# Weights converted in 8 units, one FFN product also on GpSimd, tiles 0 to 2 visited in a snake, v halves by DMA, two blocks' y in one pair of banks, and a new order of all tasks

## The chip, the cores and the metric

One NeuronCore of one Trainium2 chip runs the whole program. The metric is the device time of one execution in microseconds (us). The kernel before took 539.49 us (median of three runs, 539.39 to 540.33).

The engines go by short names: PE is TensorE (matmul; PEld its weight loads), DVE is VectorE, ACT is ScalarE, POOL is GpSimd, SP is SyncE, which here only issues DMAs. Each engine works through its own queue in program order, and they meet at semaphores.

## What is computed

A linear attention with a decaying state, and behind it a feed-forward network (FFN) with a rational activation. The reference, cut:

```
for t in range(S):                                   # B,H,S,D = 4,8,768,48
    cur = einsum('bhd,bhe->bhde', u * kt, vt)
    y[:, :, t] = einsum('bhd,bhde->bhe', rt, state + cur)
    state = w[..., None] * state + einsum('bhd,bhe->bhde', kt, vt)
x = y as (3072 tokens, 384)
h = x @ w_in                                         # 384 x 2048
g = (a0 + a1*h + a2*h^2 + a3*h^3) / (1 + |b0|*|h| + |b1|*h^2 + 1e-6)
out = g @ w_out                                      # 2048 x 384
```

The weights `w_in` and `w_out` come as float64, 6.3 MB each.

## The kernel before, in words

**Attention.** The tokens are cut into 24 blocks of 128 (4 sequences, 6 blocks each; block n is block n // 4 of sequence n % 4). For each block k, r and v are loaded (`Lk`, `Lr`, `Lv`), k is scaled by inverse powers of the decay (`sk`), k and r are transposed on PE (`tk`, `tr`) and evicted (`tke`, `tre`). PE then makes the scores and the state update in two banks (`akv`), with matmuls on 64x64 quarters of the array. DVE masks the scores (`ae`, four per block), the state is moved on (`kvm`, `kvx`, `ca`), PE makes y (`y`) and DVE adds it to a bonus term (`ye`). The bonus term is built by `ba`, `bb`, `bs`, `bv`. `LV` makes a copy of v whose halves of 64 rows stand exchanged, either by an engine from v in SBUF or by a DMA from DRAM (line 451).

**FFN.** Two blocks are a tile of 256 tokens; there are 12. y is transposed (`x`) and split into a high and a low part (`xh`, `xl`). The hidden width of 2048 is cut into 16 pieces of 128, and a slice is four such pieces of one tile: 48 slices, the last one split (list `SL`, line 35). For a slice, `f1` makes h (36 matmuls of 256 columns, into PSUM buffer h0 or h1), ACT makes `z`, `t`, `q`, `ln`, `ex`, DVE makes `u3`, `hi`, `p`, `d`, `lo`, each one pass over 128x1024 elements, and `f2` multiplies the high and low part of g with `w_out` (two halves of 12 matmuls of 384 columns). `p` (line 683) is (q + QE) * hi, `d` uses it, and `lo` is the last that reads the slice's PSUM buffer, so the slice two further on that uses the buffer waits for `lo`. Runs of slices that follow one another in one tile (`VISIT`, line 44) collect in one PSUM bank per half; at the end of a run `os` evicts it, the first time as a copy, later by adding to the sum in SBUF (lines 735 to 745).

**Weights.** Each weight is turned from float64 into a high and a low float32r part by `cl` (load), `c0` (scale the upper word, line 378), `cu` (the lower word), `c2` (shift, line 385), `c3` (sign, line 388), `cr` (integer add, line 392), `ch` (high part, line 397) and `co` (low part, line 400). This is done in 28 pieces: 12 of `w_in` (128x512) and 16 of `w_out` (128x384). Tiles 0 to 2 are worked together on the first half of the hidden width, since the later weights are not there yet.

**The order.** A string `ORDER` (lines 49 to 162) names every task, its engine (D, A, G for POOL, P, S) and its buffer; the program issues them in this order, which is so the order of each engine's queue. `warm.n` issues n matmuls of 512 bf16 columns whose result is not used (line 782). At the end a flag (`flag`, `flagt` on PE, `flagm` on DVE, lines 354 and 355) says whether a general path must run instead; every engine loads it at line 891 and branches at line 892.

```
for task in ORDER.split():
    task, e, slot = re.fullmatch(r"(.+)([A-Z])((?:[a-z]+\d)*)", task).groups()
    name, *at_ = task.split(".")
    here[:] = re.findall(r"[a-z]+\d", slot)
    FN[name](ENG[e], *at_)
```

Of the kernel before, what the change touches and what calls it, by code (L numbers as in the profile page):

```python
# [49 lines left out]
pad.0G mskG pad.1G Lr.1A wS cl_D ctrA plGos0 pow.0D inv.2Dta0 inv.3D inv.0D warm.10P turn.0.1Ppa0 pow.1D turn.2.1P turn.3.1P  # L50
inv.1D Lk.0Slx0 Lr.0S pow.2D pow.3D tr.0Ph0 turn.1.1P tab.1A sk.0D warm.4P tk.0Ph1 tre.0D Lv.0Sldv0 LV.0.0Avx0 LV.0.1A Lv.1Sldv1
cl.3S c0.3A c2.3Dpa1 Lk.1Slx1 Lk.2Slx2 sk.1G tr.1Ppa0 tke.0A warm.1P akv.0Ph0 tre.1D c3.3D w128D ba.1Dm0 ba.0Gm1 tk.1Ph1 cl.1S
tke.1A c0.1A cu.1A Lr.2S warm.3P akv.1Ph1 pad.2G ae.0.1.0D sk.2G tk.2Ppa0 kvm.0D kvx.0D ae.0.0.0D ae.0.1.1D ae.1.0.0D ae.0.0.1D
warm.2P warm.13P y.0Ph0 ae.1.1.0D ba.2Dm2 cl.0S c0.0A tke.2A kvm.1D c2.1Dpa1 c2.0Dpa0 c3.0D c3.1D uwS bb.1G Lk.3Slx0 cl.2S cu.2A
cu.0A Lr.3S Lv.2Sldv2 c0.2A ae.1.0.1D kvx.1D bb.0G bb.2G LV.1.0Avx1 LV.1.1A cr.1Gta1 ch.1A bs.0Ddt0 bv.0G bs.1Ddt1 ae.1.1.1D
tr.2Ppa0 c2.2Dpa1 c3.2D tre.2D ye.0D sk.3G tk.3Ppa1 warm.1P akv.2Ph1 cl.8S cr.0Gta2 c0.8A LV.2.0Avx2 LV.2.1A c2.8Dpa0 ae.2.1.0D
bs.2Ddt0 c3.8D Lk.4Slx1 cl.4S cl.21S co.1G cr.2Gta3 ch.0A kvm.2A c0.4A cu.3A kvx.2D ch.2A c2.4Dpa0 ae.2.0.0D ae.2.0.1D c3.4D
# [111 lines left out]
def tile_linear_attention_rational_ffn(ctx, tc, r, k, v, w, u, w_in, w_out, a, b, out):  # L169
# [195 lines left out]
    def wo_of(j, part):  # L365
        return whole["o", j][:, part]
# [557 lines left out]
```

## Time and profile before

| | |
|---|---|
| median of three runs | 539.49 us |
| span of the profiled execution, first to last instruction (the time that the profile has of it) | 536.8 us |
| PE busy | 516.8 us (96%), 6174 matmuls |
| DVE busy | 472.0 us (88%), 654 instructions |
| ACT busy | 345.9 us (64%), 421 instructions |
| POOL busy | 149.0 us (28%), 166 instructions |
| share of the chain that ended last: PE, DVE, DMA | 79%, 9%, 3% |

A median run is 2.7 us longer than the profiled span. Busy time of an engine is the union of its instructions; the time from one matmul's start to the next one's start is shorter than the duration shown for one, since matmuls are pipelined, and DVE's instructions overlap a little too. A row of a group ends with the idle time ahead of the group and what ended it.

### The profile page before, as it was taken

What the parts mean: (1) busy time and instruction counts of PE and PEld (TensorE: products, weight loads), DVE (VectorE), ACT (ScalarE), POOL (GpSimd) and SP (SyncE); (2) the same over time, 40 slices, a digit from 0 to 9 for tenths busy, and PEclk for the clock granted to TensorE, in tenths of its full rate; (3) what the DMA queues carried; (4) which work ended last, traced back from release to release, by engine and by line L of the source; (5) the groups of instructions that cost most, each with busy time, mean ns of one, the idle gap of its engine ahead of it and who ended that gap; (6) DMA issues with size and microseconds to landing.
All of it is one profiled execution on the core that took longest, in us unless ns stands there. A gap on an engine that the chain in (4) does not pass through costs nothing.

```text
span 536.8 us, 14270 instructions
## 1 busy us (share of the span) xinstructions
PE 516.8 (96%) x6174; PEld 488.5 (91%) x6174; DVE 472.0 (88%) x654; ACT 345.9 (64%) x421; POOL 149.0 (28%) x166
## 2 busy tenths in 40 slices
PE   7689999999999999999999999999999999999996
PEld 4466799989999999999999999999999999999995
DVE  6889999999999999898899898899769898798675
ACT  3578999876765655743566565575665746656663
POOL 3788954858513030014320210005002000000000
PEclk9999999999999999999999999999999999999999
DMA  9999910600043310161212420022000010010101
GB/s 196 267 267 321 236 54 2 129 1 3 0 83 60 80 29 1 34 126 23 49 32 46 94 63 5 16 45 50 16 18 1 2 42 2 1 46 1 44 2 35
DMA packets 90358, 33.93 MB, mean 63 GB/s; under 512 B 83504, under 2 KB 86704, under 8 KB 90288
## 3 DMA queue, kind: packets, MB, share of 16 engines
q1 hardware_dynamic: 88960, 32.36, 24.6%
q8 instruction: 50, 0.82, 0.6%
q10 hardware_dynamic: 1328, 0.59, 0.4%
q14 instruction: 20, 0.16, 0.1%
HBM read 28.22 MB, written 4.72 MB: 61 GB/s over the span
## 4 chain that ended last, share of the span: by engine, by line
PE 79%; DVE 9%; DMA 3%; ACT 2%; issue 1%; SPq 0%; DVEq 0%; ACTq 0%
PE h L618 34%; PE o L622 11%; PE o L624 11%; PE o L623 11%; DMA swi<-in_moe_w_in_dram 3%; PE y L569 2%; PE akv L519 2%; PE y L567 2%; PE akv L523 1%; PE tk L497 1%; PE tr L497 1%; PE x L593 1%; DVE q L685 1%; DVE h L676 1%; DVE g L681 1%
## 5 line engine op out<-in xcount | busy, mean ns | idle before, releaser
L618 PE MATMUL h<-xthi,wi 128*128 128x256 f32 x1152 | 216.0, 282 | 1.4 <-DVE l L694 1.1
L618 PEld LDWEIGHTS h<-xthi,wi 128*128 128x128 f32 x1152 | 180.3, 188 | 3.6 <-issue 1.2
L618 PE MATMUL h<-xtlo,wi 128*128 128x256 f32 x576 | 160.7, 279 | 0.0
L622 PE MATMUL o<-wo,g 128*128 128x384 f32 x384 | 133.1, 347 | 0.0
L623 PE MATMUL o<-wo,g 128*128 128x384 f32 x384 | 129.1, 336 | 0.0
L624 PE MATMUL o<-wo,l 128*128 128x384 f32 x380 | 128.1, 337 | 0.4 <-DVE l L694 0.3
L618 PEld LDWEIGHTS h<-xtlo,wi 128*128 128x128 f32 x576 | 108.3, 188 | 0.0
L664 ACT ACTIVATE z<-h,off,root 128x1024 f32<-128x1024 f32 (+1 forms) x48 | 57.3, 1194 | 65.4 <-PE h L618 55.3
L681 DVE SCALAR_TENSOR_TENSOR g<-h,sig,z 128x1024 fp32r<-128x1024 f32 (+1 forms) x48 | 61.0, 1271 | 28.4 <-ACT z L672 27.9
L655 ACT ACTIVATE q<-h 128x1024 f32<-128x1024 f32 (+2 forms) x50 | 49.3, 989 | 53.2 <-PE h L618 42.1
L622 PEld LDWEIGHTS o<-wo,g 128*128 128x128 f32 x384 | 72.2, 188 | 1.0
L624 PEld LDWEIGHTS o<-wo,l 128*128 128x128 f32 x380 | 71.4, 188 | 1.0 <-DVE l L694 1.0
L623 PEld LDWEIGHTS o<-wo,g 128*128 128x128 f32 x384 | 72.3, 188 | 0.0
L668 ACT ACTIVATE z<-q,sig 128x1024 f32<-128x1024 f32 (+1 forms) x48 | 54.9, 1144 | 26.6 <-DVE h L676 25.6
L676 DVE SCALAR_TENSOR_TENSOR h<-z,sig,h 128x1024 f32<-128x1024 f32 (+1 forms) x48 | 61.1, 1272 | 7.1 <-ACT z L664 3.8
L685 DVE SCALAR_TENSOR_TENSOR q<-q,sig,g 128x1024 f32<-128x1024 f32 (+2 forms) x50 | 64.4, 1289 | 1.4
L689 DVE SCALAR_TENSOR_TENSOR h<-h,sig,q 128x1024 f32<-128x1024 f32 (+2 forms) x50 | 62.4, 1248 | 1.3
L659 ACT ACTIVATE q<-q,off,root 128x1024 f32<-128x1024 f32 (+2 forms) x50 | 60.4, 1207 | 0.8
L694 DVE TENSOR_TENSOR l<-h,z 128x1024 fp32r<-128x1024 f32 (+1 forms) x48 | 58.1, 1211 | 2.3 <-DVE h L689 0.5
L478 POOL TENSOR_TENSOR m<-rh,kn 128x384 f32<-128x384 f32 x20 | 23.8, 1193 | 113.7 <-DMA kn<-in_k_dram 66.2
L672 ACT ACTIVATE z<-z 128x1024 f32<-128x1024 f32 (+1 forms) x48 | 50.5, 1052 | 1.5
L530 DVE TENSOR_TENSOR sc<-akv,mask 64x256 f32<-64x256 f32 x96 | 40.4, 421 | 5.1 <-PE akv L523 3.2
(132 smaller groups left out, 672.7 us busy)
## 6 DMA issues: line engine op xcount, KB each, us to landing
swo<-in_moe_w_out_dram SPq DMA_DIRECT2D x16, 384.0 KB, 6.6
swi<-in_moe_w_in_dram SPq DMA_DIRECT2D x12, 512.0 KB, 6.6
kn<-in_k_dram SPq DMA_DIRECT2D x24, 192.0 KB, 4.1
vn<-in_v_dram SPq DMA_DIRECT2D x24, 192.0 KB, 3.8
rh<-in_r_dram SPq DMA_DIRECT2D x23, 192.0 KB, 3.6
out_dram<-os SPq DMA_DIRECT2D x22, 192.0 KB, 2.1
vx<-in_v_dram SPq DMA_DIRECT2D x26, 48.0 KB, 2.7
out_dram<-os ACTq DMA_DIRECT2D x2, 192.0 KB, 2.8
```

The lines of the kernel that those rows point to most:

```text
L618: nc.tensor.matmul(o, wi_of(j, cc, part), x_[:, cc], start=(n == 0), stop=(n == 3 * NCC - 1))
L622: nc.tensor.matmul(o, hi, wo_of(j, HI), start=first, stop=False)
L623: nc.tensor.matmul(o, hi, wo_of(j, LO), start=False, stop=False)
L624: nc.tensor.matmul(o, lo, wo_of(j, HI), start=False, stop=last)
L659: nc.scalar.activation(g["q"], g["q"], AF.Square, scale=RB, bias=KB)
L664: nc.scalar.activation(g["t"], g["h"], AF.Square, scale=RA, bias=KA)
L668: nc.scalar.activation(g["z"], g["q"], AF.Ln, bias=QE)
L676: nc.vector.scalar_tensor_tensor(g["h"], g["t"], KAP, g["h"], op0=ALU.add, op1=ALU.mult)
L681: nc.vector.scalar_tensor_tensor(g["hi"], g["h"], c0, g["z"], op0=ALU.add, op1=ALU.mult)
L685: nc.vector.scalar_tensor_tensor(g["q"], g["q"], qe, g["hi"].bitcast(F32), op0=ALU.add, op1=ALU.mult)
L689: nc.vector.scalar_tensor_tensor(g["h"], g["h"], c0, g["q"], op0=ALU.add, op1=ALU.subtract)
L694: nc.vector.tensor_mul(g["lo"], g["h"], g["z"])
```

## The change

Five things, and a new `ORDER`:

1. Weight conversion in 8 units (w_in and w_out in four groups of 512 hidden columns each; even units are w_in, odd w_out), each 1536 columns wide. A task names unit, part and number of parts: thirds of 512 or halves of 768 columns. `c0` may run on POOL, `ch` and `co` on DVE.
2. A task `qa` on ACT adds QE to q, and `p` of slices 0, 1, 15, 19 and 40 is then a plain product on POOL.
3. `SL` visits (2,0) (2,4) (1,4) (0,4) (0,8) (0,12) instead of (2,0) (0,4) (1,4) (2,4) (0,8) (0,12), a snake through tiles 0 to 2.
4. A task `Y` makes y of both blocks of a tile in one pair of banks, used for tiles 4 to 10.
5. More of the `LV` halves come by DMA.

Tasks by engine in the two orders, where they differ (counted from the strings):

```
               before             after
c0             A 28               A 9, G 8
cu             A 28               A 17
c2, c3         D 28 each          D 24 each
cr             G 28               G 16
ch             A 28               A 15, D 1
co             G 28               G 15, D 1
cl             S 28               S 20
p / qa         D 50 / -           D 45, G 5 / A 5
os             A 20, D 16         A 16, D 16
LV             A 16, D 6, S 26    A 4, D 8, S 36
kvm            A 2, D 22          A 4, D 20
xh             A 15, D 9          A 18, D 6
tke            A 20, D 4          A 19, D 5
sk             D 4, G 20          D 7, G 17
bb / bv        D 3, G 21 / D 7, G 17     D 4, G 20 / D 6, G 18
ca             D 4, G 16          D 7, G 13
y / Y          P 24 / -           P 10 / P 7
warm           81 matmuls         34 matmuls
```

The flag's tasks `flagt` and `flagm` stand ahead of slice 48 before, and at the very end after. The core of the diff:

```diff
-    (0, 0, 4), (1, 0, 4), (2, 0, 4), (0, 4, 4), (1, 4, 4), (2, 4, 4), (0, 8, 4), (0, 12, 4), (1, 8, 4),
+    (0, 0, 4), (1, 0, 4), (2, 0, 4), (2, 4, 4), (1, 4, 4), (0, 4, 4), (0, 8, 4), (0, 12, 4), (1, 8, 4),
...
+hi.1Dta5
+f2.0.1P cr.2.0.2Gta4 Lv.8Sldv2 c3.3.2.3D os.0.0Aos1 p.1G f1.2.0Ph1 cl.4.1.3S ch.2.0.2A ch.2.1.2A cu.6.1.2A Lr.6S co.2.1.2G co.2.0.2G
+c2.3.1.3Dpa1 f1.2.1P f1.2.2P f1.2.3P c2.3.0.3Dpa0 c3.3.1.3D c3.3.0.3D d.1D c0.4.0.2G t.2Ata0 z.2Ata2 lo.1Dta3 f1.3.0Ph0 Lr.7S q.2A
...
+hi.49D d.48D p.49D lo.48D d.49D f2.47.0P f2.47.1P lo.49D f2.48.1P f2.49.1P f2.48.0P f2.49.0P os.49.1Aos2 od.11.1A os.49.0Aos4 od.9.1S
+flagtPh0 od.11.0A flagmD
...
+    QW = NCC * CW
+    def cols(k, m):
+        return ts(k, QW // m)
...
+    def cv_exp(c, k, m, e):
+        top = c["top"][:, cols(k, m)].bitcast(F32)
+        if e is nc.scalar:
+            e.activation(top, top, AF.Copy, scale=2.0 ** -112)
+        else:
+            e.tensor_scalar(top, top, 2.0 ** -112, None, op0=ALU.mult)
...
+    def cv_round(c, k, m):
+        bits = ew.tile([P, QW // m], I32, tag=here[0], name=f"b{c['tag']}_{k}")
+        nc.gpsimd.tensor_tensor(bits, c["top"][:, cols(k, m)], c["low"][:, cols(k, m)], op=ALU.add)
+        c["f", k] = bits.bitcast(F32)
...
+    def yy_pe(f):
+        both = pair("y", 2 * f)
+        wide = state[2 * f].pop("yw", None)
+        for x in range(2):
+            n, o = 2 * f + x, x * NP * D
+            state[n]["y"] = tuple(bank[:, o : o + NP * D] for bank in both)
+            if wide is not None:
+                state[n]["yw"] = wide[:, :, o : o + NP * D]
+            y_pe(n)
...
-    def ew_p(s, qe=QE):
+    def ew_qa(s):
         g = gs[s]
+        nc.scalar.activation(g["q"], g["q"], AF.Identity, bias=QE)
+
+    def ew_p(s, qe=QE, e=None):
+        g = gs[s]
+        if e is nc.gpsimd:
+            e.tensor_mul(g["q"], g["q"], g["hi"].bitcast(F32))
+            return
         nc.vector.scalar_tensor_tensor(g["q"], g["q"], qe, g["hi"].bitcast(F32), op0=ALU.add, op1=ALU.mult)
```

## Rows read from the trace of the kernel before

**Rows 1.** Three stretches; columns: stretch, length, each engine's busy time, granted clock, DMA, GB/s
```profile
core 0: us, PE busy (x) PEld busy (x) DVE busy (x) ACT busy (x) POOL busy (x), PEclk, DMA share, GB/s
0.00:125.50 125.50, 111.38 (x1495) 92.58 (x1495) 115.47 (x198) 98.82 (x164) 84.97 (x100) 0.99 0.60 158
125.50:242.20 116.70, 116.70 (x1358) 114.30 (x1351) 109.15 (x152) 71.07 (x73) 29.36 (x30) 1.00 0.22 48
242.20:531.50 289.30, 288.70 (x3333) 281.67 (x3331) 246.72 (x306) 175.86 (x186) 34.64 (x38) 1.00 0.12 28
```

**Rows 2.** Instructions in order of time, DVE and PE, around the start of slice 8
```profile
124.30 1.22 DVE L694 TENSOR_TENSOR l<-h,z 128x1024 fp32r<-128x1024 f32 x1
...
125.45 0.22 PE L567 MATMUL y<-vn,sc 64*64 64x48 f32 x1
125.60 0.39 PE L618 MATMUL h<-xthi,wi 128*128 128x256 f32 x1
```

**Rows 3.** Instructions in order of time, PE, the last matmul
```profile
531.19 0.33 PE L624 MATMUL o<-wo,g 128*128 128x384 f32 x1
```

**Rows 4.** Instructions in order of time, PE, 47 to 53 us: fillers, transposes
```profile
47.22 2.32 PE L782 MATMUL idle_bank<-wones 128*128 128x512 bf16 x10
...
50.92 0.63 PE L497 MATMUL tk<-ident,kh 128*128 128x128 f32 x4
```

**Rows 5.** DVE's groups by shape, first 126 us: count, busy us, mean ns
```profile
L530 DVE TENSOR_TENSOR sc<-akv,mask 64x256 f32<-64x256 f32 x32 | 13.5, 421 | 2.5 <-PE akv L523 1.9
...
L685 DVE SCALAR_TENSOR_TENSOR q<-q,sig,g 128x1024 f32<-128x1024 f32 x7 | 9.6, 1366 | 0.1
...
L385 DVE TENSOR_SCALAR c<-swo 128x384 int32<-128x384 int32 x15 | 8.2, 554 | 0.5 <-issue 0.2 <-ACT swo L378 0.2
...
L385 DVE TENSOR_SCALAR c<-swi 128x512 int32<-128x512 int32 x12 | 8.0, 685 | 0.1
...
L745 DVE SCALAR_TENSOR_TENSOR os<-o,sig,os 128x384 f32<-128x384 f32 x4 | 2.4, 605 | 0.0
```

**Rows 6.** Instructions in order of time, DVE, two neighbours
```profile
54.01 0.69 DVE L385 TENSOR_SCALAR c<-swi 128x512 int32<-128x512 int32 x1
54.60 0.55 DVE L580 TENSOR_TENSOR m<-y,m 128x384 f32<-128x384 f32 x1
```

**Rows 7.** POOL by line: low parts (min/median/max ns), integer add (count, busy, mean ns)
```profile
L400 POOL TENSOR_TENSOR wo<-bwo,wo x16: 992/1018/2006, 40.5 to 139.3; 128x384 fp32r<-128x384 f32 x16
L400 POOL TENSOR_TENSOR wi<-bwi,wi x12: 1267/1295/2253, 24.5 to 110.7; 128x512 fp32r<-128x512 f32 x12
...
L392 POOL TENSOR_TENSOR bwi<-swi 128x512 int32<-128x512 int32 x12 | 12.5, 1040 | 5.9 <-PE o L624 3.8 <-issue 1.1 <-POOL bwo L392 0.9
```

**Rows 8.** Instructions in order of time, DVE and POOL side by side near 110 us
```profile
109.92 1.89 DVE L685 SCALAR_TENSOR_TENSOR q<-q,sig,g 128x1024 f32<-128x1024 f32 x1
110.70 2.25 POOL L400 TENSOR_TENSOR wi<-bwi,wi 128x512 fp32r<-128x512 f32 x1
```

**Rows 9.** Instructions in order of time, DVE, the end of slice 1
```profile
73.54 1.21 DVE L694 TENSOR_TENSOR l<-h,z 128x1024 fp32r<-128x1024 f32 x1
```

**Rows 10.** Three more stretches, columns as in the first group
```profile
0.00:10.00 10.00, 6.61 (x27) 3.26 (x28) 5.14 (x16) 3.30 (x7) 2.17 (x15) 1.00 0.93 177
20.00:30.00 10.00, 6.34 (x127) 4.38 (x126) 7.71 (x16) 6.44 (x15) 7.53 (x8) 0.83 0.94 236
0.00:74.75 74.75, 62.96 (x989) 46.02 (x990) 66.06 (x133) 54.44 (x105) 54.88 (x71) 0.98 0.90 241
```

**Rows 11.** DMA issues: count, KB each, median us to landing
```profile
vx<-in_v_dram SPq DMA_DIRECT2D x26, 48.0 KB, 2.7
```

**Rows 12.** The flag on DVE in order of time; line 892 on PE (ns, start us)
```profile
523.15 0.27 DVE L354 TENSOR_REDUCE oks<-flagt 1x1 f32<-1x128 f32 x1
523.45 0.14 DVE L355 CAST okf<-oks 1x1 int32<-1x1 f32 x1
...
L892 PEldq COMPARE_BRANCH  x1: 3322/3322/3322, 531.1 to 531.1; - x1
```

**Rows 13.** Instructions in order of time, PE, after the longest early wait
```profile
24.16 1.02 PE L497 MATMUL tk<-ident,kh 128*128 128x128 f32 x4 [3.65 <-DVE swi L388]
```

More of the change, by code (lines that the diff above doesn't have):

```diff
@@ L54 @@
[L54 to L57, printed above, removed]
@@ L358, in tile_linear_attention_rational_ffn @@
     HI, LO = 0, 1
-    pieces = []
+    units = []
     whole = {}
+    QW = NCC * CW
     def wi_of(j, cc, part):
-        return whole["i", j * P // CW, cc][:, part, ts(j % (CW // P), P)]
+        return whole["i", j * P // CW][:, part, ds(cc * CW + j * P % CW, P)]
     def wo_of(j, part):
-        return whole["o", j][:, part]
-    def piece(name, src, n):
-        pieces.append({"name": name, "src": src, "n": n, "tag": "w" + "_".join(map(str, name))})
-    def cv_load(c, e):
-        st = cst.tile([P, c["n"], 2], I32, tag=c["tag"], name="s" + c["tag"])
-        e.dma_start(st.rearrange("p n two -> p (n two)"), c["src"])
-        c["top"], c["low"] = st[:, :, 1], st[:, :, 0]
@@ L390, in cv_round @@
-    def cv_round(c):
-        bits = ew.tile([P, c["n"]], I32, tag=here[0], name="b" + c["tag"])
-        nc.gpsimd.tensor_tensor(bits, c["top"], c["low"], op=ALU.add)
-        c["f"] = bits.bitcast(F32)
-    def cv_hi(c):
-        c["w"] = whole[c["name"]] = cst.tile([P, 2, c["n"]], F32R, tag=c["tag"], name=c["tag"])
-        nc.scalar.copy(c["w"][:, HI], c["f"])
-    def cv_lo(c, e):
-        e.tensor_sub(c["w"][:, LO], c["f"], c["w"][:, HI].bitcast(F32))
+        return whole["o", j * P // CW][:, part, ts(j % (CW // P), DM)]
@@ new lines, in cols, with cv_load @@
+    def cols(k, m):
+        return ts(k, QW // m)
+    def cv_load(c, k, m, e):
+        if "st" not in c:
+            c["st"] = cst.tile([P, QW, 2], I32, tag=c["tag"], name="s" + c["tag"])
+            c["top"], c["low"] = c["st"][:, :, 1], c["st"][:, :, 0]
+        dst = c["st"][:, cols(k, m)].rearrange("p n two -> p (n two)")
+        kind, g = c["name"]
+        if kind == "i":
+            e.dma_start(dst, wi32[ts(k, P), ts(g, 2 * CW)])
+        else:
+            j = CW // P // m
+            rows = ds((g * m + k) * j * P, j * P)
+            e.dma_start(dst.rearrange("p (j n) -> p j n", j=j), wo32[rows, :].rearrange("(j p) n -> p j n", p=P))
@@ L408, in tile_linear_attention_rational_ffn @@
     for g in range(FF // CW):
-        for cc in range(NCC):
-            piece(("i", g, cc), wi32[ts(cc, P), ts(g, 2 * CW)], CW)
-        for j in range(g * (CW // P), (g + 1) * (CW // P)):
-            piece(("o", j), wo32[ts(j, P), :], DM)
+        for kind in "io":
+            units.append({"name": (kind, g), "tag": f"w{kind}{g}"})
     rh, kh, rt, sc, vs = ([], [], [], [], [])
@@ L464, in pair @@
         if here[0][0] == "h":
-            wide = state[n][nm + "w"] = ps_h.tile([P, GW], F32, tag=here[0], name=f"{nm}{n}")
+            wide = ps_h.tile([P, GW], F32, tag=here[0], name=f"{nm}{n}")
+            state[n][nm + "w"] = wide.rearrange("t (x c) -> t x c", x=2)
             return wide[:, 0:512], wide[:, 512:1024]
```

261 lines of the change are left out of this document (133 added, 128 removed).

## The prediction

> **What bounds the kernel now.** I read three things in order: where TensorE (PE) is full, who holds it up before that, and what it does at the end. Busy time by stretch [rows 1]: from 125.5 us on PE is busy for all of 116.7 us and for 288.7 of 289.3; only the first 125.5 us have room (111.4, and filler matmuls are in it). In that stretch VectorE (DVE) is busy 115.5 of 125.5. The seam is exact [rows 2]: DVE finishes the low half `lo` of slice 6 at 124.30 + 1.22 = 125.5, which frees the PSUM buffer h0, and PE starts slice 8 (into h0) at 125.60, right behind the last y matmul. From there to its last matmul [rows 3] PE needs 531.19 + 0.33 - 125.60 = 405.9 us with next to no waiting. So the time is: DVE's ordered work up to `lo` of slice 6 (DVE is an in-order queue), then 405.9 us of PE, then an end of 536.8 - 531.5 = 5.3 us. The sum below is made against this execution's span of 536.8; the median, 539.49, is 2.7 above it, which I add.
>
> **The filler.** The order holds 81 filler matmuls (`warm`) before and 34 after, all before slice 2; ten take 2.32 us [rows 4], so 47 fewer are 10.9 us of PE. I cost this at nothing by itself: they sit in gaps where PE waits for something else. It says only that the room exists.
>
> **DVE's work ahead of slice 8.** I count the DVE tasks that stand ahead of `lo.6` in both orders and price them by DVE's groups [rows 5].
> - Weight conversion, shift and sign: 27 pieces each (12 of 512 columns, 15 of 384) become 21 of 512. Shift: 12 x 0.685 + 15 x 0.554 - 21 x 0.685 = 2.1; the sign step taken at the same price, so 4.3 together. About 1.2 of it is gone for good (24 pieces in all instead of 28), 3.1 only comes later.
> - The product `p` of slices 0 and 1 goes to GpSimd (POOL): 2 x 1.37 = 2.7.
> - The snake makes slices 2 and 3 one output run, and 5, 6 and 7 one: four evictions fewer in all, two of them on DVE ahead of this point: 2 x 0.605 = 1.2.
> - A bonus product, a scaling of k and an x copy leave DVE for POOL or ScalarE (ACT), 128x384 like the 0.554 row: 1.7.
> - Four small ones (two state copies to ACT, a masked copy and a reduction to later), priced as the masked copy: 4 x 0.42 = 1.7.
>
> Sum 11.6 us in 23 instructions. Neighbours overlap: a shift of 0.69 us is followed after 0.59 [rows 6], so 23 x 0.10 = 2.3 comes off: **9.3 us**. Below: 0 if the later work comes back, above: 11.6.
>
> **POOL, the new wait.** `d` of slices 0 and 1 stands in DVE's queue and now waits for POOL's `p`; behind `d.1` stand the rest of slice 1, conversions and attention. POOL's multiply of 1024 columns is not in the trace. Its two-input form takes 1.018 for 384 columns and 1.295 for 512 [rows 7]: 0.00216 a column, so 1.295 + 512 x 0.00216 = 2.4 us. Low end 1.3 (the 512 row), high end twice the 2.25 that one such instruction took beside DVE's `p`, 4.5 [rows 8]: the two did not run side by side there. I take 2.4, since most 512 rows lie at the low value. The Trainium skill (GPSIMD Engine Reference, 4.1 Engine selection) says to keep elementwise work on VectorE because GpSimd needs about twice as long for two inputs; by it `p` stays on DVE and my sum loses 2.7. The rows agree on the factor (2.4 against 1.37), but DVE is the full engine here and POOL is not [rows 1]. The scaling `c0` on POOL is not shown either: the integer add of 512 columns takes 1.04 [rows 7], so a half of 768 columns 1.5 (low 0.8, as if one input cost half; high 1.9, by the float form).
> Is POOL there in time? Up to 74.75, the end of `lo.1` (73.54 + 1.21 [rows 9]), it was busy 54.9 us [rows 10]. Ahead of `p.1` and with it the new order has, against the old up to `lo.1`: `c0` +5.5 (a third and three halves), `p` +4.8, a scaling of k +1.1, low parts 12 to 4 pieces -7.2, rounding 14 to 6 -4.5, a carry -0.6: about -0.9, so 54.0. DVE has 9.1 us less ahead of `lo.1` (shift and sign 35 to 26 pieces 3.9, two `p` 2.7, five others 2.5), 1.6 of it overlap, and `d.1` starts two passes, 2.4 us, before `lo.1` ends: it would reach `d.1` at 74.75 - 7.5 - 2.4 = 64.8. So POOL may idle 10.8 us before it is late. It idled 19.9 up to 74.75, 7.8 of it in the first 10 us [rows 10], when nothing had landed; the new order gives it a bonus product and a conversion there, and ACT, for whose roundings it waited later, has nine copies of v and 14 scalings fewer ahead. Lateness 0 to 9 us; I take **1**, near the low end, as most of the old idle has lost its cause.
>
> **The rest.** ACT's `qa` is one more pass over slices 0, 1, 15, 19 and 40; ACT is busy 98.8 of the first 125.5 us [rows 1] and loses 14 scalings, so 0, and at most a pass, 1.3, for each of the first two without that cover. `p` of 15, 19 and 40 costs PE nothing while `f2` trails its slice by one or more; without it 1 to 2 us each. The v halves by DMA: 26 to 36 loads of 48 KB that land in 2.7 us [rows 11]; two per block 0 to 3 instead of ACT copies. On SP, `LV.3.0` and `LV.4.0` wait for y of blocks 0 and 1, and behind them queue r of block 5 and the weights of units 6 and 2; with the DMA engines' share at 0.90 [rows 10] there is a backlog while SP waits, so 0, and 1 to 3 us if y.1 is late. Joint y: the 64x64 stretches on PE go from 44 to 37, 3 of them after slice 8; from the last y to the next `f1` it takes 0.15 [rows 2]; with the entry alike at most 0.3 a stretch, of which I take 0.2, so 0.6 less (0 to 0.9). The later DVE work (3.1 + some of the small ones) falls in the stretch where DVE idles 7.5 us [rows 1].
> The flag: its turn and reduction move behind the last `f2`. Before, the reduction started at 523.15, the cast ended at 523.59, and PE's last branch started at 531.1 and took 3.3 us [rows 12]. Now no engine can read the flag before last matmul + about 0.3 (turn) + 0.44: PE's and DVE's ends come later by about **0.9**; between 0 (hidden by the output's landing) and 1.5.
>
> **The sum.** Slice 8 at 125.6 - 9.3 + 1 = 117.3; last matmul 117.3 + 405.9 - 0.6 = 522.6; end 5.3 + 0.9: span 528.8, 8.0 less. With 2.7: **531.5 us**.
>
> **The rivals.**
> - *The deferred work comes back* (0.12). Conversions and small ones, 5 us, are only moved behind slice 8, where DVE is busy 109.2 of 116.7 [rows 1]. If its 7.5 idle us there are not usable, as each is a wait in the middle of a slice, 5 return: 536.5. For: both engines are nearly full. Against: PE had no wait there before.
> - *The clock falls* (0.10). After a wait of 3.65 us PE's next four transposes took 1.02 us, 0.63 elsewhere [rows 4, 13], and the mean granted clock of 20 to 30 us was 0.83, so one spell at 1.2 instead of 2.4 GHz [rows 10]. With 47 filler matmuls gone, gaps between the first blocks could do this several times. About 1 us lost in such a spell, four or five: 536.5. Against: the new order's long waits are fewer, and DVE sets the pace there. The Trainium skill (TensorE: Matmul & The Clock Gate, Part 1) says that the idle array is throttled by default and activity releases it; the trace agrees, by that row.
> - *POOL is in time and all edges fit* (0.12): no lateness, 11.6 instead of 9.3, so 528.2, and up to 525.5 if DVE's 10.0 idle us in the head [rows 1] shrink by a quarter as well.
> - *PE waits elsewhere* (0.05): the head shrinks on DVE but PE is held by the loads (the DMA engines are 0.90 busy up to 74.75 [rows 10]), so the fillers become idle time: 539.5, no change.
> - *POOL becomes the bound: slower* (0.11). If it idles as long as before (19.9), `p.1` comes at 73.9, 9.1 late; at the dear ends of `p` (+4.2) and `c0` (+1.5) 14.8 late. Then slice 8 starts at 125.6 - 9.3 + 14.8 = 131.1, 5.5 later than before, and with -0.6 + 0.9 the time is 545. It decides from a lateness of 10 us on.
>
> **Chances.** My forecast has 0.50 (528 to 535). Some 0.2%, 1.1 us, is what a measurement of this kernel can tell from no change. Faster: 0.50 + 0.12 + 0.12 + 0.10 = 0.84; same 0.05; slower 0.11. The range leaves out the last two and the very best: 525.5 to 538.5, which covers lateness 0 to 8, conversions at either end, and the two milder rivals.
>
> **What would show it.** Right: in the stretches of the changed kernel PE is full from about 117 us on, slice 8 starts within 0.2 us of `lo.6`, and the 405 us behind it are the same within 2. `p` on POOL at 2.3 to 2.6 us and `d.1` on DVE idle before it for under 2 us. The branch on PE ends about 0.9 later behind the last matmul. Wrong: DVE idle for several us behind POOL at `d.0` or `d.1`; spells at the lower clock between 12 and 30 us; PE idle between 126 and 500; `lo.18` no more than 5 us earlier than before.

## The result and the profile after

The changed kernel takes **545.98 us** (median of four runs, 544.46 to 546.75) against 539.44 us for the kernel before beside it: ratio **1.0126** (95% interval 1.0100 to 1.0152), 6.5 us slower. Forecast were 531.5 us and a range of 525.5 to 538.5, so sign and size were both wrong. The profiled execution took 546.25 us with a span of 542.8.

The stretches of the changed kernel, with the columns of [rows 1]: up to the end of `lo.6`, up to and from the start of slice 8, and three slices of 10 us in the head:

```profile
core 0: us, PE busy (x) PEld busy (x) DVE busy (x) ACT busy (x) POOL busy (x), PEclk, DMA share, GB/s
0.00:126.10 126.10, 105.66 (x1388) 92.61 (x1388) 106.58 (x175) 85.91 (x115) 98.96 (x87) 0.93 0.63 160
...
128.00:246.70 118.70, 117.38 (x1351) 115.05 (x1352) 108.25 (x137) 73.58 (x74) 32.65 (x28) 1.00 0.22 43
246.70:536.50 289.80, 287.78 (x3326) 279.64 (x3324) 250.28 (x334) 174.85 (x182) 33.51 (x32) 1.00 0.13 30
...
10.00:20.00 10.00, 6.23 (x81) 4.17 (x80) 4.54 (x9) 4.75 (x11) 9.70 (x13) 0.70 0.98 230
...
30.00:40.00 10.00, 8.54 (x151) 7.67 (x152) 7.61 (x18) 5.24 (x9) 8.00 (x10) 0.83 0.90 222
70.00:80.00 10.00, 6.76 (x34) 6.50 (x35) 9.42 (x9) 7.18 (x8) 10.00 (x8) 0.66 0.63 185
```

Three things are to be seen. DVE's work ahead of `lo.6` did shrink, from 115.5 [rows 1] to 106.6 us; but DVE now idles 126.1 - 106.6 = 19.5 us there, where it idled 10.0. The granted clock is 0.70, 0.83 and 0.66 in three slices (its two levels are 1.2 and 2.4 GHz, that is 0.5 and 1), where the kernel before had one dip ahead of slice 8, 0.83 in 20 to 30 us [rows 10]. And from slice 8 on PE has (118.7 - 117.4) + (289.8 - 287.8) = 3.3 us of idle time, where it had 0.6.

PE's longest waits behind slice 8 (us in total, times, longest):

```profile
PE h L640 <- DVE l L723: 1.2, 2, 0.6
PE y L591 <- DVE vs L558: 0.7, 1, 0.7
PE y L589 <- DVE sc L540: 0.6, 1, 0.6
```

DVE's waits up to `lo.6`, in the same form:

```profile
DVE c2wi L393 <- POOL swi L385: 3.7, 1, 3.7
DVE wcol L288 <- DMA wraw<-in_w_dram: 3.3, 2, 1.9
DVE sc L540 <- ACT vs L414: 3.0, 2, 2.4
DVE sc L540 <- PE akv L533: 2.4, 4, 1.4
```

No single wait holds the 9.5 us by which DVE's idle time grew (that of `wcol` is old: 3.0 us before the change). Instructions in order of time (start, duration; idle time and releaser in brackets): the first chain, the end of slice 1, the seam and the flag.

```profile
9.34 1.00 POOL L488 TENSOR_TENSOR m<-rh,kn 128x384 f32<-128x384 f32 x1 [7.11 <-DMA kn<-in_k_dram]
...
11.38 1.54 POOL L385 TENSOR_SCALAR swi<-swi 128x512 f32<-128x512 f32 x1
...
12.95 0.69 DVE L393 TENSOR_SCALAR c2wi<-swi 128x512 int32<-128x512 int32 x1 [3.74 <-POOL swi L385]
...
13.69 1.01 POOL L484 TENSOR_TENSOR kh<-kn,wkn 128x384 f32<-128x384 f32 x1
...
14.76 1.12 PE L507 MATMUL tk<-ident,kh 128*128 128x128 f32 x4 [3.77 <-POOL kh L484]
...
16.65 1.13 PE L529 MATMUL akv<-rt,kt 64*64 64x64 f32 x32
17.56 1.05 PE L533 MATMUL akv<-vn,kh 64*64 64x48 f32 x32
...
19.10 0.88 DVE L540 TENSOR_TENSOR sc<-akv,mask 64x256 f32<-64x256 f32 x2 [2.37 <-ACT vs L414]
...
67.99 2.42 POOL L712 TENSOR_TENSOR q<-q,g 128x1024 f32<-128x1024 f32 x1
...
70.45 1.29 DVE L718 SCALAR_TENSOR_TENSOR h<-h,sig,q 128x1024 f32<-128x1024 f32 x1 [1.26 <-POOL q L712]
...
124.85 1.23 DVE L723 TENSOR_TENSOR l<-h,z 128x1024 fp32r<-128x1024 f32 x1
126.11 0.43 DVE L540 TENSOR_TENSOR sc<-akv,mask 64x256 f32<-64x256 f32 x1
...
126.68 0.33 PE L591 MATMUL y<-vs,rt 64*64 64x48 f32 x8 [0.58 <-DVE sc L540]
...
128.04 0.38 PE L640 MATMUL h<-xthi,wi 128*128 128x256 f32 x1 [0.21 <-DVE swo L397]
...
536.11 0.34 PE L646 MATMUL o<-wo,g 128*128 128x384 f32 x1
...
536.59 0.28 DVE L349 TENSOR_REDUCE oks<-flagt 1x1 f32<-1x128 f32 x1 [1.71 <-PE flagt L346]
```

Block 0 stands in a row behind POOL: bonus product, scaling of the first weight third, mask, and only then the scaling of k for which PE's `tk.0` waits 3.77 us. Behind that wait the clock is down: `akv.0` takes from 16.65 to 18.61, 1.96 us, where it took 1.14 in the kernel before (PE in order of time there):

```profile
10.80 0.69 PE L519 MATMUL akv<-rt,kt 64*64 64x64 f32 x32
11.31 0.63 PE L523 MATMUL akv<-vn,kh 64*64 64x48 f32 x32
```

So DVE's wait of 2.37 us, which is listed under ACT, is for the most part one for PE: ACT's copy in between only takes from 18.68 to 19.00. Slice 8 (128.04) no longer starts right behind `lo.6` (126.1), as in [rows 2], but 1.9 us later: `y.7` in front of it waits for one of its own block's masked scores (`ae.7.1.1`), which the new order puts behind `lo.6` on DVE.

POOL's groups by shape (count, busy us, mean ns):

```profile
L712 POOL TENSOR_TENSOR q<-q,g 128x1024 f32<-128x1024 f32 x5 | 12.0, 2407 | 19.6 <-DVE g L703 19.6
L401 POOL TENSOR_TENSOR bwi<-swi 128x768 int32<-128x768 int32 x8 | 11.7, 1476 | 3.8 <-ACT sig L264 2.2 <-DVE swi L397 1.6
...
L385 POOL TENSOR_SCALAR swi<-swi 128x768 f32<-128x768 f32 x3 | 6.8, 2282 | 0.0
```

`p` takes 2.41 us on POOL (2.4 forecast). The scaling of 768 columns takes 2.28, above the high end of 1.9 that I had given it. The Trainium skill (GPSIMD Engine Reference, 4.1 Engine selection) calls one-input work on GpSimd roughly line-rate. The trace differs, and the measurement decides: DVE's shift, also of one input, passes 512 of these columns in 0.69 us, POOL's scaling of 512 takes 1.54, and that of 768, in place on every other word, is 1.5 times as dear as the two-input integer add of as many columns (1.48).

### The profile page after: what moved, and what is told of

It is laid out like the page before. It is cut to its first block, busy times and chain, and to the rows that moved or that the text cites. A ratio compares the mean times of both kernels' runs of the same rounds, so it can differ in the third digit from the quotient of the medians.

```text
span 542.8 us, 14082 instructions
## 1 busy us (share of the span) xinstructions
PE 512.0 (94%) x6127; PEld 488.4 (90%) x6127; DVE 467.4 (86%) x650; ACT 336.4 (62%) x371; POOL 166.6 (31%) x148
## 4 chain that ended last, share of the span: by engine, by line
PE 67%; DVE 15%; POOL 6%; ACT 6%; issue 3%; SPq 1%; DMA 1%; DVEq 0%; ACTq 0%; POOLq 0%
PE h L640 30%; PE o L646 9%; PE o L644 9%; PE o L645 9%; PE akv L529 2%; DVE sc L540 2%; DVE h L698 2%; DVE q L714 2%; PE akv L533 2%; DVE h L718 2%; DVE g L703 2%; PE tk L507 2%; POOL wi L411 2%; PE y L589 1%; PE y L591 1%
## 5 line engine op out<-in xcount | busy, mean ns | idle before, releaser
L640 PE MATMUL h<-xthi,wi 128*128 128x256 f32 x1152 | 225.1, 287 | 7.2 <-DVE l L723 5.6
L640 PEld LDWEIGHTS h<-xtlo,wi 128*128 128x128 f32 x576 | 109.6, 190 | 0.0
L677 ACT ACTIVATE q<-h 128x1024 f32<-128x1024 f32 (+1 forms) x48 | 48.7, 1014 | 64.0 <-PE h L640 51.4
L686 ACT ACTIVATE z<-h,off,root 128x1024 f32<-128x1024 f32 (+2 forms) x50 | 58.5, 1170 | 42.5 <-PE h L640 32.4
L703 DVE SCALAR_TENSOR_TENSOR g<-h,sig,z 128x1024 fp32r<-128x1024 f32 (+2 forms) x50 | 62.0, 1239 | 23.4 <-ACT z L694 22.9
L698 DVE SCALAR_TENSOR_TENSOR h<-z,sig,h 128x1024 f32<-128x1024 f32 (+2 forms) x50 | 62.0, 1240 | 6.7 <-ACT z L686 3.7
L718 DVE SCALAR_TENSOR_TENSOR h<-h,sig,q 128x1024 f32<-128x1024 f32 (+1 forms) x48 | 61.4, 1279 | 6.9 <-POOL q L712 5.7
L502 POOL TENSOR_TENSOR m<-vn,dt 128x384 f32<-128x384 f32 x18 | 15.2, 845 | 149.7 <-DVE dt L498 129.5
L714 DVE SCALAR_TENSOR_TENSOR q<-q,sig,g 128x1024 f32<-128x1024 f32 (+1 forms) x43 | 59.3, 1379 | 1.4
L681 ACT ACTIVATE q<-q,off,root 128x1024 f32<-128x1024 f32 (+1 forms) x48 | 59.2, 1232 | 0.8
L694 ACT ACTIVATE z<-z 128x1024 f32<-128x1024 f32 (+2 forms) x50 | 51.3, 1027 | 1.4
```

The source lines that it names most:

```text
L640: nc.tensor.matmul(o, wi_of(j, cc, part), x_[:, cc], start=(n == 0), stop=(n == 3 * NCC - 1))
L681: nc.scalar.activation(g["q"], g["q"], AF.Square, scale=RB, bias=KB)
L686: nc.scalar.activation(g["t"], g["h"], AF.Square, scale=RA, bias=KA)
L698: nc.vector.scalar_tensor_tensor(g["h"], g["t"], KAP, g["h"], op0=ALU.add, op1=ALU.mult)
L703: nc.vector.scalar_tensor_tensor(g["hi"], g["h"], c0, g["z"], op0=ALU.add, op1=ALU.mult)
L714: nc.vector.scalar_tensor_tensor(g["q"], g["q"], qe, g["hi"].bitcast(F32), op0=ALU.add, op1=ALU.mult)
```

## The experiments

Every kernel ran beside the kernel before on the same chip; ratios are to that, with 95% intervals. The groups stood on different chips (e12 and e13 too), so between groups I compare ratios. Diffs show the tasks of the order, the unchanged ones between them left out.

**How much one execution tells.** The changed kernel again, no edit.

> The changed kernel once more, unchanged, for a second profile and the spread. If the head's timing varies from one execution to the next (the run with the flag moved had the same head and started slice 8 at 125.6, not 128.0): slice 8 anywhere from 125 to 129, while the stretch from slice 8 to the last matmul of the FFN is again 408.2 to 408.9. If the trace of the changed kernel is typical: slice 8 at 127.5 to 128.5. Time 544.5 to 546.5.

Measured: 543.40 us (541.85 to 547.12), ratio 1.0097 (1.0070 to 1.0125), below the time expected. Its second profile, stretches as above:

```profile
0.00:123.20 123.20, 102.20 (x1388) 89.17 (x1388) 107.42 (x175) 86.15 (x115) 98.77 (x87) 0.96 0.64 163
...
125.20:533.50 408.30, 405.00 (x4675) 394.63 (x4675) 358.42 (x470) 248.32 (x254) 66.18 (x60) 1.00 0.15 34
```

The head varies (slice 8 at 125.2 here, DVE idle 15.8), the 408.3 us behind it do not. The spans of the changed kernel run from 538.7 to 544.0 in six runs; those of the kernel before from 535.8 to 538.1 in sixteen beside them. So a single profile of the head is good to some 3 us, and I go by medians, and by kernels based on the one before, whose spread is small.

**POOL's share.**

```diff
e1: -c0.0.1.3G c0.6.1.2G ... c0.7.0.2G  +c0.0.1.3A c0.6.1.2A ... c0.7.0.2A   (all eight)
e2: -qa.0A p.0G ... qa.40A p.40G        +p.0D ... p.40D                     (all five)
e3: both
e4: -c0.0.1.3G ... sk.0G                +c0.0.1.3A ... sk.0D c2.0.1.3D
e6: e4, with tk.0P tke.0A ahead of c0.0.1.3A c0.0.2.3A, and c2.0.2.3D c3.0.2.3D behind kvx.0D
b1: the kernel before, -p.kD +qa.kA p.kG for k = 0, 1, 15, 19, 40
```

> All ten scalings c0 that stood on POOL go to ACT, at the same places of the order. Theory 1 (POOL is the wait of the head: its scalings cost 2.27 us for 768 columns and 1.54 for 512, 17.4 us in all): DVE's wait of 3.7 us before the first shift falls below 1.5, p.1 on POOL starts before 66 us instead of 67.99, DVE's d.1 does not wait, slice 8 starts at 122 to 125 instead of 128.0, time 540 to 543. Theory 2 (the new order with fewer filler matmuls is the cause: gaps on TensorE and half-clock spells, whatever POOL does): slice 8 stays at 127 to 129, spells stay, 545 to 547. If ACT, 14 us fuller, becomes the wait of the head: 547 or more.

> The product p of slices 0, 1, 15, 19 and 40 goes back to DVE and ACT's pass qa falls away. Theory 1 (POOL): the wait of d.1 (1.26 us) and the TensorE gap of 3.7 us before slice 3 mostly go, with the half-clock spell of 72 to 79 us; against it DVE has 2 x 1.38 more ahead of slice 8: slice 8 at 125.5 to 127.5, the 408.4 us behind it lose 1 to 2 as d.15, d.19 and d.40 wait no more: 542 to 544.5. Theory 2 (order and clock): slice 8 at 128 to 130 by DVE's added 2.8, time 546 to 548.5.

> Both: scalings c0 on ACT and p on DVE, so POOL's share is as before the change. Theory 1 (POOL): the sum of the two, slice 8 at 121 to 125, 538 to 542. Theory 2 (the order and the clock): 545 or more, with TensorE gaps over 1.5 us in the first 40 us still there.

> Only the first chain is mended: the scaling of the first weight piece (c0.0.1.3) goes to ACT and the scaling of the first k (sk.0) back to DVE, ahead of the first shift; everything later stays on POOL. Theory 1a (the head is lost in its first 15 us, when block 0 stands behind POOL): tk.0 on TensorE starts at 9.5 to 11.5 instead of 14.76, no half clock at 14 us, slice 1 starts 3 to 4 us earlier than 51.7, slice 8 at 124 to 126, 541.5 to 544. Theory 1b (POOL's later load decides: p.1 behind three scalings): the first blocks are earlier but p.1 is not, slice 3 stays within 1 us of 73.1 and slice 8 within 1 us of 128.0: 545 to 546.5.

(The text for the first says ten scalings; the order has eight.) Measured, with the median span and the median of what a run's time has beyond its span:

| | time us | ratio | span us | beyond it |
|---|---|---|---|---|
| changed kernel, first four runs | 545.98 | 1.0126 (1.0100 to 1.0152) | 542.6 | 3.4 |
| changed kernel, c1 | 543.40 | 1.0097 (1.0070 to 1.0125) | 540.7 | 3.1 |
| e1 | 544.64 | 1.0102 (1.0080 to 1.0123) | 541.8 | 2.9 |
| e2 | 546.18 | 1.0116 (1.0082 to 1.0150) | 544.5 | 1.7 |
| e3 | 543.88 | 1.0088 (1.0058 to 1.0117) | 542.1 | 1.7 |
| e4 | 544.10 | 1.0107 (1.0087 to 1.0127) | 542.1 | 2.0 |

None comes near 1 (e2 falls in Theory 2's range, the others between the ranges), and none has a span shorter than c1's: what fell is the time beyond the span. In e1 DVE waits no more than 1.0 us at a time for the first scalings, but 2.8 for PE's `tr`, and idles 19.7 us as before. With POOL relieved of everything that was new for the FFN (e3), slice 8 still starts at 126.8, and DVE idles 124.9 - 109.6 = 15.3 us up to `lo.6`. Theory 1, POOL as the wait of the head, explains 2 us of time at most, and no part of the span that these runs can tell. In e4 the profile has slice 8 at 124.0, but it is of the quickest of its six runs; the median gains less.

> On top of the first chain (sk.0 on DVE, c0.0.1.3 on ACT, as in the run before): on ACT the first key transpose's copy tke.0 goes ahead of the first two scalings, which wait for weights, and DVE's shift and sign of the second piece go behind block 0's attention. If block 0 is late because weight conversions that wait for their transfers stand ahead of it in the in-order queues: akv.0 on TensorE at 12 to 13.5 us instead of 14.3, DVE's idle time up to lo.6 falls from 14.2 to 11 to 13, slice 8 at 122 to 123.5 (124.0 without), 542 to 543.5. Rival (the later stretches wait for the weights and for POOL, and early time saved is waited out again before slice 1): slice 8 at 123.8 to 124.5 or later, 543.5 to 545.

Measured: 545.68 us, ratio 1.0132 (1.0111 to 1.0153): a miss, slice 8 at 126.8. Putting block 0 ahead by hand on two queues only moved the wait.

> The kernel before with one part of the change alone: the product p of slices 0, 1, 15, 19 and 40 on POOL, with ACT's pass qa, at the old places of the old order. Theory A (a saving on DVE is worth its time where nothing is taken from POOL's readiness): lo.6 2 to 3 us earlier than 125.5, span 533.5 to 536, ratio 0.994 to 0.999. Theory B (what the old order leaves no room for comes back as a wait: each d right behind its p waits for POOL's 2.4 us, as the order was not made for it): DVE waits 1 to 3 us at each of the five, slice 8 at 125 to 128, and TensorE waits behind slices 15, 19 and 40; ratio 1.000 to 1.010.

Measured: 542.36 us, ratio 1.0064 (1.0050 to 1.0078): `p` on POOL, with `qa` on ACT, makes the old order slower by 3.4 us, and nothing else was changed: Theory B. Its first stretch, up to `lo.6`:

```profile
0.00:127.60 127.60, 111.34 (x1495) 92.20 (x1495) 112.89 (x196) 100.86 (x166) 88.92 (x102) 0.99 0.60 155
```

The first product on POOL, in order of time:

```profile
50.72 2.38 POOL L690 TENSOR_TENSOR q<-q,g 128x1024 f32<-128x1024 f32 x1 [3.65 <-ACT wi L397]
```

Two of DVE's waits in the same stretch:

```profile
DVE m L580 <- POOL m L492: 1.4, 1, 1.4
...
DVE h L696 <- POOL q L690: 0.5, 1, 0.5
```

DVE's work falls by 2.6 us (115.5 to 112.9; 2.7 forecast), its idle time rises by 4.7. `d.0` hardly waits; `ye.4`, whose bonus product on POOL is queued behind `p.0`, waits 1.4. Who is queued behind the new instruction costs more than the instruction's own reader.

**The clock.**

```diff
e7: e4, +warm.28P f1.3.0
e8: the changed kernel, -warm.5P tk.0 +warm.19P tk.0; +warm.6P akv.2; +warm.60P f1.3.0
b3: the kernel before, -warm.13P y.0  -warm.6P akv.4  -warm.10P x.3  -warm.7P y.4  -warm.9P y.5
```

> On top of the first chain mended (sk.0 on DVE, c0.0.1.3 on ACT): 28 filler matmuls of 128 columns in TensorE's gap of 3.4 us ahead of slice 3. Theory 2 (the clock): no half-clock spell between 66 and 80 us, slices 3 to 4 take 2 us less, slice 8 at 122.0 to 123, 541.5 to 542.5. Rival (DVE sets the pace there): the spell goes, and slice 8 stays at 123.6 to 124.4, 543.5 to 544.5. Slower if the fillers are still running when lo.1 is done: 545.

Measured: 544.76 us, ratio 1.0100 (1.0082 to 1.0118): inconclusive. The narrow fillers ended some 2 us ahead of slice 3, and the clock still fell there (0.83 in 70 to 80 us).

> The changed kernel with filler matmuls back in its three longest head gaps alone: 14 of 512 columns ahead of tk.0 (a gap of 4.1 us), 6 ahead of akv.2 (1.6) and 60 of 128 columns ahead of slice 3 (3.7). Theory 2 (the clock): the spells of half clock at 14, 31 and 72 us go, the mean granted clock is 0.99 or more instead of 0.981 to 0.987, and the time falls by 1.5 to 3 us, to 543 to 544.5. Rival (DVE's waits set the head's pace and the clock only follows the gaps): the clock rises, the time stays within 1 us of the changed kernel's in this call.

Measured: 541.59 us, ratio 1.0064 (1.0041 to 1.0087), mean clock of the profiled run 0.993 against 0.981 and 0.989: 1.8 us less than the changed kernel beside it, as Theory 2 had it, though the intervals overlap, and in its profile DVE idles 15.9 us up to `lo.6`, as in c1's. By itself e8 settles nothing.

> The kernel before with 45 of its 81 filler matmuls taken out (those ahead of y.0, akv.4, x.3, y.4 and y.5), nothing else. Theory 2 (the clock: the fillers hold TensorE's granted clock up, so taking them out costs time): the mean clock falls from 0.995 to 0.985 to 0.99, a second and third half-clock spell between 20 and 60 us, the time 1 to 3 us longer, ratio 1.002 to 1.006. Rival (they only filled waits): the clock may fall, the ratio is 0.998 to 1.001.

Measured: 542.16 us, ratio **1.0068** (1.0051 to 1.0085): 45 filler matmuls taken out of the kernel before, nothing else, cost 3.7 us, more than the 1 to 3 expected; the rival is out. Three of its stretches:

```profile
0.00:128.90 128.90, 106.34 (x1450) 92.45 (x1450) 115.09 (x198) 98.95 (x164) 84.80 (x100) 0.92 0.58 154
20.00:30.00 10.00, 6.53 (x125) 4.29 (x123) 7.68 (x16) 7.33 (x16) 7.94 (x9) 0.66 0.99 239
...
50.00:60.00 10.00, 7.91 (x94) 7.10 (x95) 9.08 (x13) 9.08 (x20) 6.07 (x6) 0.57 0.89 232
```

Two of DVE's waits in the first 126 us:

```profile
DVE sc L530 <- PE akv L523: 3.6, 3, 2.0
DVE m L580 <- PE y L567: 1.3, 3, 0.9
```

The clock of 50 to 60 us is 0.57: behind gaps that the fillers had held, PE works at the lower level. DVE's work is the same (115.1), its idle time 13.8 instead of 10.0, and slice 8 starts 3.4 us later: DVE waits 3.6 us for PE's a and kv, where it was 1.9 [rows 5], and 1.3 for its y. No run moves the clock without moving fillers; that the clock does it is read from these rows and from `akv.0` in the changed kernel. The Trainium skill (TensorE: Matmul & The Clock Gate, HAM oscillation) describes this for another kernel: waits between bursts of matmuls bring the clock down, and the next burst starts at the lower rate. The trace agrees. Its Part 1 puts the penalty of the ramp at a kernel's start below 1 per cent of a typical span. What b3 prices is another thing, spells later in the head and the waits behind them: 0.68 per cent, 3.7 us, where the whole loss is 6.5.

**The flag.**

```diff
e5: the changed kernel, +flagtP f2.45.0 ... +flagmD p.47 ... -flagtP od.11.0A -flagmD
b2: the kernel before, -flagtP f2.45.0 ... -flagmD p.47 ... +flagtP od.11.0A +flagmD
```

> The changed kernel with the flag's turn and reduction back at their old place, ahead of the last matmuls. If the end is as I worked it out, the time from the last matmul of the FFN to the end of the span falls from 6.4 us to 5.2 to 5.6 and the time to 544.5 to 545.3; rival (the end is set by the fetch of code behind the branch on TensorE and by DVE, wherever the flag is turned): 6.2 or more, time 545.5 to 546.5.

> The kernel before with the flag's turn and reduction behind the last matmuls, nothing else. By my working 0.9 us more at the end (0 to 1.5), ratio 1.000 to 1.003. If the late read exposes the fetch of code behind the branch as in four of the profiles (an end of 8.1 to 8.4 us instead of 6.4): 1.5 to 3.0 us more, ratio 1.003 to 1.006.

Measured: e5 542.68 us, ratio 1.0068 (1.0054 to 1.0081), an end of 6.1 us instead of 6.4 and 6.5 in the two profiles of the changed kernel, short of the 5.2 to 5.6 expected. Its median span, 540.7, is that of c1; what it gains on c1 lies beyond the span (2.0 instead of 3.1). b2 540.04 us, ratio **1.0026** (1.0015 to 1.0038), 1.4 us slower. The end of b2 in order of time:

```profile
531.53 0.34 PE L624 MATMUL o<-wo,g 128*128 128x384 f32 x1
...
532.44 0.27 DVE L354 TENSOR_REDUCE oks<-flagt 1x1 f32<-1x128 f32 x1
```

PE's branch behind it (ns; the last figures are its start):

```profile
L892 PEldq COMPARE_BRANCH  x1: 3542/3542/3542, 533.5 to 533.5; - x1
```

The branch starts 1.6 us behind the last matmul's end, where it started 0.4 ahead of it [rows 3, 12]; the end grows from 5.3 to 538.5 - 531.9 = 6.6. In three runs with the late flag (e4, e6, e7; the text above says four) it was 8.1 to 8.4.

**The stretch behind slice 8.**

```diff
e9: -Y.5P ... f1.17.3P  +f1.17.3P Y.5P;  -Y.7P ... f1.22.0P  +f1.22.0P Y.7P
e10: e4 + all c0 on ACT + the flag as in e5 + e9
```

> The changed kernel with the joint products Y.5 and Y.7 one pass of f1 later on TensorE. If the 2.5 us by which the stretch behind slice 8 grew are waits of a joint y for the attention of its second block on DVE (0.7 and 0.6 us here): that stretch takes 407.0 to 407.6 instead of 408.4 us, time 1 us below the changed kernel's. Rival (what DVE does late makes the next step wait as long): 408.2 to 408.6.

> The mended parts together: flag ahead of the last matmuls, all scalings c0 on ACT, sk.0 on DVE ahead of the first shift, Y.5 and Y.7 later. If their effects add (about 3 + 1 + 1.5 + 1 us): 539 to 541, as fast as the kernel before or nearly. If they are the same slack counted several times: 541.5 to 543.

Measured: e9 547.51 us, ratio 1.0150 (1.0132 to 1.0167); e10 544.74, 1.0112 (1.0097 to 1.0127). Both misses: the stretch behind slice 8 takes 412.2 us in e9 and 410.8 in e10. With `Y.5` later, slices 16 to 20 take 45.0 us instead of 45.2; with `Y.7` later, PE waits at slice 22 (PE in order of time, e9):

```profile
274.11 0.34 PE L646 MATMUL o<-wo,l 128*128 128x384 f32 x1
277.44 0.36 PE L640 MATMUL h<-xthi,wi 128*128 128x256 f32 x1 [2.99 <-DVE vs L558]
```

That pass needs the bank that block 14's products hold until DVE has taken them (`kvx.14`), and `Y.7` was what PE did meanwhile. The 0.7 and 0.6 us waits of the joint y stand in front of longer ones.

**Together.**

```diff
e11: e8 + the flag as in e5
e12: e4 + all c0 on ACT + the flag as in e5,
     -warm.5P tk.0 +warm.13P tk.0; -warm.2P akv.0 +warm.8P akv.0; +warm.6P akv.2; +warm.45P f1.3.0
e13: e12, +warm.5P y.0; +warm.4P tr.2; -warm.1P akv.3 +warm.5P akv.3
e14: e13, -lo.6D ae.7.1.1D +ae.7.1.1D p.6D; -Y.5P f1.17.3P +f1.17.3P Y.5P
```

> The changed kernel with the head fillers and the flag at its old place together. If the two terms are separate (clock 2 us, flag 1 to 2 us): 539 to 540.5, ratio 1.000 to 1.004. If one contains the other: 541 to 542.5.

> The changed kernel with sk.0 back on DVE ahead of the first shift, all scalings c0 on ACT, the flag at its old place, and fillers in the head's gaps (8 more of 512 columns ahead of tk.0, 6 ahead of akv.0, 6 ahead of akv.2, 45 of 128 columns ahead of slice 3). If POOL's part, the clock's part and the flag's part add: 537 to 539, ratio 0.996 to 1.001, slice 8 at 121.5 to 123.5. If the rest of the order (the 2.5 us behind slice 8, DVE's waits in the first 40 us) keeps it: 539.5 to 541.5.

> The mix of the run before (sk.0, scalings, flag, fillers) with 13 more filler matmuls in the three gaps over 1 us that its profile still had: 5 ahead of y.0, 4 ahead of tr.2 and 4 more ahead of akv.3. If the clock holds the remainder: no half-clock spell in the first 80 us, mean clock 0.997 or more, spans of 534 to 537 in most runs instead of 534 to 541, time 536.5 to 538.5, ratio 0.995 to 0.999. Rival (DVE's waits on the order hold it): the clock rises, the time stays at 538.5 to 540.5, ratio 1.000 to 1.004.

> The same with two steps of the order moved: ae.7.1.1 ahead of slice 6's p on DVE, so that y.7 need not wait behind lo.6, and the joint Y.5 one pass later on TensorE. If such single waits are worth their length: slice 8 0.4 to 0.7 us earlier against lo.6's end than in the run beside it, the stretch behind slice 8 0.2 to 0.5 us shorter, in all 0.5 to 1 us less than that run. Rival (each wait covers the next): within 0.3 us of it.

Measured: e11 540.75 us, ratio 1.0044 (1.0020 to 1.0068), between its two forecasts. e12 539.63, 1.0025 (1.0001 to 1.0050), in its second range, spans from 534.4 to 541.5 us. e13 **537.23, 0.9981 (0.9969 to 0.9993)**, in its first range, spans from 534.6 to 537.1: 13 more filler matmuls, and nothing else, take 2.4 us off the median (beside each the kernel before took 538.49), close the spread, and give a kernel 0.2 per cent faster than the one before. e14, a miss, 537.61, 0.9986 (0.9972 to 1.0001): `ae.7.1.1` ahead of `lo.6` brings slice 8 0.4 us closer to it, and a new wait of 0.9 at 178 us takes that back. The stretches of e13:

```profile
0.00:119.80 119.80, 109.03 (x1466) 92.63 (x1466) 105.22 (x176) 91.55 (x123) 80.93 (x78) 1.00 0.65 168
...
70.00:80.00 10.00, 9.92 (x69) 9.39 (x70) 9.85 (x11) 9.83 (x11) 4.29 (x5) 1.00 0.79 212
...
121.80:530.20 408.40, 405.04 (x4675) 394.67 (x4675) 358.68 (x472) 248.55 (x254) 66.57 (x60) 1.00 0.15 34
```

Three of its DVE's waits up to `lo.6`:

```profile
DVE h L698 <- ACT q L677: 2.7, 3, 1.4
DVE kh L484 <- ACT wkn L321: 2.5, 1, 2.5
DVE sc L540 <- ACT vs L414: 2.2, 1, 2.2
```

With the clock at 1.00 throughout, `lo.6` ends at 119.8, 5.7 us earlier than before the change. DVE still idles 14.6 us, and half of that is for ACT. One of these waits, 2.2 us, stood in the changed kernel too, there for PE. Here PE's `akv.0` is done at 16.36, and ACT's copy `kvm.0`, a task that the change took from DVE, stands behind a scaling that ends at 18.38 (e13, PE and ACT in order of time):

```profile
15.73 0.63 PE L533 MATMUL akv<-vn,kh 64*64 64x48 f32 x32
...
18.29 0.29 ACT L414 COPY vs<-akv 128x192 f32<-128x192 f32 x1
```

A wait that is mended uncovers the next. The 408.4 us behind slice 8 are what they were in every version that kept the new order there: 2.5 more than before.

## Why the prediction was wrong

The working against the first profile, step by step:

| step | forecast us | measured us | off by |
|---|---|---|---|
| DVE's work up to `lo.6` | 115.5 - 9.3 = 106.2 | 106.6 | +0.4 |
| DVE's idle time up to `lo.6` | 10.0 + 1 = 11.0 | 19.5 | +8.5 |
| from `lo.6` to slice 8 | 0.1 | 1.9 | +1.8 |
| slice 8 to the last matmul | 405.3 | 408.4 | +3.1 |
| the end | 6.2 | 6.4 | +0.2 |
| outside the span | 2.7 | 3.45 | +0.75 |
| time | 531.5 | 546.25 | +14.75 |

The largest miss is DVE's idle time. Three terms of the prediction stand behind it: the fillers at nothing, the lateness at 1 us, the scaling at 1.5.

- **DVE's work**: right, 23 instructions and their overlap included. In b1 `p` too was worth what it was costed at.
- **"I cost this at nothing by itself"**, of the fillers: the step that failed. That sentence looked at PE's time, which is indeed free there, and not at what the filler keeps up. It stood in the text as a rival, *the clock falls*, with the right mechanism, at 5 us and 0.10. Measured alone on the kernel before it is 3.7 us, and fillers alone moved e12 to e13 by 2.4. From e10 to e13 the ratio falls by 0.0131, 7 us; these two differ by fillers and by `Y.5` and `Y.7`, which cost e10 2.4 us behind slice 8 (410.8 against 408.4). So fillers are worth some 4.6 us in the new order, an estimate from these runs. I had argued that "DVE sets the pace there": DVE's waits for PE in b3 show that in the attention blocks the two take turns.
- **"Lateness 0 to 9 us; I take 1"**: the mechanism was there (`d.1` waited 1.26 us), but idle time came from chains that I had not priced: block 0 behind four POOL tasks (3.7 us), `akv.0` at the lower clock behind that (2.4), in b1 `ye` behind POOL. I summed engines' busy times against their idle times; neither tells the order in which four in-order queues hand one block on. Relieving POOL of `p` and the scalings gave back 2 us of time at most and left the spans as they were, so the rival *POOL becomes the bound*, the one that ended on the slower side (545), had the number nearly right and the cause mostly wrong.
- **The scaling on POOL at 1.5**: mis-sized; 2.28 for 768 columns, outside the range given (0.8 to 1.9). The four ahead of `p.1` take 1.54 + 3 x 2.28 = 8.4 us, where the sum had 5.5.
- **The seam "within 0.2 us of `lo.6`"**: wrong by 1.8. I carried the old seam over without reading what `y.7` waits for in the new order: it is the masked copy that I had credited with 0.42 us for standing later.
- **Joint y "0.6 less"**: PE's work behind slice 8 did fall a little (405.4 to 405.2), but its idle time rose by 2.7. Of the waits listed above, one of the two for `lo` is old; the other is slice 9's for `lo.7`, behind conversions that come later now, and then there are `Y.5` and `Y.7`; the rest are 0.3 or less each. So the rival *the deferred work comes back* is seen at 0.6 us. POOL's `p` of 15, 19 and 40 is not the cause: with it on DVE (e2) the stretch takes 408.8. Whether another order would be rid of these waits, the runs do not settle; moving `Y.5` and `Y.7` was not the way.
- **The flag "+0.9"**: right in kind, a little small; the end grew by 1.3 in b2, its time by 1.4.

The parts on their own, fillers (3.7 in the old order; 1.8 and 2.4 in the new), flag 1.4, `p` in the old order 3.4, cannot be added to 6.5, since each moves the same chains. Fillers and flag put back together, with the first chain and the scalings, took the changed kernel from 1.0126 and 1.0097 to 0.9981; `p` stayed on POOL. The forecast is not met even so: in e13 slice 8 starts at 121.8 instead of 117.3, and the stretch behind it takes 408.4 instead of 405.3.

Open: the time outside the span. It is 1.7 to 1.8 us in all runs of the kernel before that are listed with their span, and in e13; 3.4 in the four runs of the changed kernel, 3.1 to 3.2 in five of its six later ones and 2.0 in the sixth. So some 1.5 us of the loss stands in no trace. I added 2.7 to the span, which for the kernel before was most likely 1.7 and an execution 1 us shorter than the median. It goes with the program: 1.7 again with `p` on DVE (e2, e3), and with all scalings on ACT and the flag early (e10, e12 to e14); 2.0 in e4 to e7 and e11, 2.9 in e1, 3.2 in e9; in e8 it varies from 1.95 to 3.95 between executions. What in the program sets it stays open.

## What to carry to other kernels

Before filler matmuls are costed at nothing, look at what the granted clock does behind each gap that they leave, and who waits for PE's small matmuls there; taking fillers out of a known kernel prices that in one run. Work saved on an in-order engine is a saving only as far as the engine was busy and not waiting: price the chain (what is queued behind a moved instruction on its new engine, and who waits for that) rather than the sum. When two profiles of one kernel differ by 3 us in the head, read causes from edits of the steadier kernel.

## What was not expected of the hardware

- The scaling of 768 columns in place on every other word takes POOL 2.28 us, and the two-input integer add of as many 1.48; the plain product of 1024 columns takes 2.41.
- Within one kernel the longer spans are mostly those at a lower mean clock: in e12 541.5 and 540.8 us at 0.989 and 0.987, 534.4 and 535.9 at 0.997 and 0.998. Between kernels the spread does not follow the clock: 2.5 us in e13 (0.995 to 0.998), 5.3 in c1 (0.985 to 0.991), but 0.7 in the five runs of e5 (0.982 to 0.991).
- With the flag read late, the end was 6.3 to 6.7 us in most profiles and 8.1 to 8.4 in three; in e4 DVE's last drain came 1.8 us behind POOL's, and the trace names nothing that it waited for.
